# Loading the first activations and weights of a gated MLP in half tiles over two DMA queues

## The chip, the cores and the metric

The kernel runs on one core of one Trainium2 chip. The metric is device time in microseconds (us), lower is better; a program on one core has one value per execution.

A ratio below is the mean time of one kernel's runs over the mean of the other's runs of the same rounds on the same chip. It is therefore not quite the ratio of the medians that stand beside it. Its 95% interval is about 0.0012 to each side with five rounds, which is 0.6 to 0.7 us here. Smaller differences are not told apart by the times, only by what a profile shows.

## The reference

```
x: (1, 2048, 1024) bf16    w_gate, w_up: (1024, 3584)    w_down: (3584, 1024)
g = x @ w_gate ; u = x @ w_up
h = gelu_tanh(g) * u
out = h @ w_down
```

## The kernel before

The kernel is tuned so that TensorE never stops once it has its first operands; its products after the first unit use a scheme with fewer multiplications, which does not matter here. What matters is the head: 512 rows of x come in as four row tiles of 128 rows, are transposed by TensorE, and are multiplied with the first 256 columns of the two weights.

```
def load_x(c):                       # the x issues: 128 rows of 2048 bytes each
    for i in range(NS):              # NS = 4
        xn = slot([P, Dm], bf16, "xn")
        r0 = c * N + i * P
        nc.sync.dma_start(out=xn, in_=x2[r0 : r0 + P, :])
        ...

def load_wf(queue, k0, k1):          # first weights, a part of the contraction at a time
    for i, src in enumerate((w_gate, w_up)):
        got = queue.dma_start(out=wf[:, i, k0:k1], in_=src[k0 * P : k1 * P, 0 : 2 * P]...)
        ...

xT = new_x()
xn0 = load_x(0)
for k0, k1 in ((0, 2), (2, 5), (5, NKB)):
    load_wf(nc.sync, k0, k1)
w = load_w(1)                        # second unit's weights, 512 KB each
for ko in range(NKB):                # x's second 512 rows, transposed by the DMA
    transposing(xT, 1, ko, N)
...
keep_warm(NWARM, N)                  # matmuls on constants until x arrives
for i in range(NS):
    if i == 2:
        keep_warm(2, 2 * P)
    turn(xT, xn0, 0, i)              # 8 transposes of tile i, then a copy into xT
plain(bank[0:4], 0, range(0, 2), parts=2)
plain(bank[0:4], 0, range(2, NKB))
```

Far from the head, the second matrix product fetches its share of w_down per step, the last two steps of each pass in two DMAs:

```
def fetch73(j):
    raw[3, j] = slot([P, 2, N], bf16, "raw")
    for kh in (range(2),) if j < NJ - 2 else (range(1), range(1, 2)):
        kh = slice(kh.start, kh.stop)
        nc.sync.dma_start(out=raw[3, j][:, kh], in_=wdn[:, kh, j, N:])
```

Of the kernel before, what the change touches and what calls it, by code (L numbers as in the profile page):

```python
# [10 lines left out]
def kernel(  # L11
# [23 lines left out]
    nc = tc.nc  # L35
    ENG = mybir.EngineType
    ORDER = {ENG.SP, ENG.DVE, ENG.Pool, ENG.PE}
    P = nc.NUM_PARTITIONS
# [7 lines left out]
    x2 = x.flatten_outer_dims()  # L46
# [7 lines left out]
    NJ = NFB // 2  # L54
    N = 512
# [24 lines left out]
    wdn = w_down.rearrange("(kh j p) d -> p kh j d", kh=2, p=P)  # L80

    def slot(shape, dtype, name):
        return kpool.tile(shape, dtype, name=name, tag="k")
# [33 lines left out]
    def load_w(u, queue=nc.sync):  # L117
        f0 = u * 2 * P
        w = wpool.tile([P, 2, NKB, 2 * P], bf16, name="w")
        for i, src in enumerate((w_gate, w_up)):  # L120
            queue.dma_start(
                out=w[:, i],
                in_=src[:, f0 : f0 + 2 * P].rearrange("(ko ki) f -> ki ko f", ki=P),
            )
        return w
# [160 lines left out]
    q12, s12, q73, q4, raw = {}, {}, {}, {}, {}  # L286
# [24 lines left out]

    def fetch73(j):
        raw[3, j] = slot([P, 2, N], bf16, "raw")
        for kh in (range(2),) if j < NJ - 2 else (range(1), range(1, 2)):
            kh = slice(kh.start, kh.stop)
            nc.sync.dma_start(out=raw[3, j][:, kh], in_=wdn[:, kh, j, N:])

    def make73(j):
        rr = raw[3, j]
# [25 lines left out]
    for j in range(NJ):  # L345
        at(AT12[j], load12, j)
        at(AT12S[j], make12, j)
        at(AT73[j] - 3, fetch73, j)
        at(AT73[j], make73, j)
        at(49 + 0.65 * j, load4, j)  # L350
        at(54 + 0.55 * j, make_sa, j)
# [80 lines left out]
    ident = xpool.tile([P, P], bf16, name="ident")  # L432
    make_identity(nc, ident)

    def load_x(c):
        t = []
        for i in range(NS):
            xn = slot([P, Dm], bf16, "xn")
            r0 = c * N + i * P
            nc.sync.dma_start(out=xn, in_=x2[r0 : r0 + P, :])  # L440
            t.append(xn)
        return t

# [10 lines left out]
            out=xT[c][:, ko, :], in_=x2[r0 : r0 + N, ko * P : (ko + 1) * P]  # L454
        )

    def load_wf(queue, k0, k1):
        for i, src in enumerate((w_gate, w_up)):
            got = queue.dma_start(
                out=wf[:, i, k0:k1],  # L460
                in_=src[k0 * P : k1 * P, 0 : 2 * P].rearrange(
                    "(ko ki) f -> ki ko f", ki=P
                ),
            )
            if queue is not nc.sync:
                tc.keep_in_program_order(got)

    xT = new_x()
    xn0 = load_x(0)
    wf = wpool.tile([P, 2, NKB, 2 * P], bf16, name="w")  # L470
    for k0, k1 in ((0, 2), (2, 5), (5, NKB)):
        load_wf(nc.sync, k0, k1)
    w = load_w(1)
    for ko in range(NKB):
        transposing(xT, 1, ko, N)
# [72 lines left out]
    for ip in range(NPASS):  # L548
# [54 lines left out]
        got, nxt = {}, {}  # L603
# [52 lines left out]
```

## Time and profile before

| | before |
|---|---|
| time, median of 3 (range) | 539.89 us (539.87 to 540.21) |
| the profiled execution | 540.66 us, span 538.8 us |
| TensorE (PE) busy, share of the span | 99% |
| granted TensorE clock from 8 us on | 1.00 |
| fourth x tile landed | 6.99 us |
| first matmul on x | 7.49 us |

The chain of work that ended last, of the kernel before (start in us, length in us, what). It shows where time can be won at all.

```profile
2.12 4.87 DMA xn<-in_x_dram
...
7.04 0.62 PE bank L447 x8
7.66 0.22 PE bank L111 x2
...
7.91 527.77 PE bank L111 x2366
...
535.71 0.58 ACT st L412
```

From 7.91 us to the last copy at 535.71 us the chain is nothing but matmuls. Only the time ahead of 7.91 us can be shortened: the issue and landing of the fourth x tile, its eight transposes (L447), and the wait for w_up.

The x issues by tile, of the kernel before (engine, operation, count, then the length in ns: least, median, most; SPq is SyncE's sequencer):

```profile
L440 SPq DMA_DIRECT2D xn<-in_x_dram x4: 392/420/432, 0.7 to 2.1; - x4
```

The engines' busy times in short stretches, of the kernel before; the last two columns are what is read here, the mean busy share of the 16 DMA engines (it can pass 1, as a packet's whole time counts in the stretch in which it starts) and the GB/s that they moved:

```profile
1.50:2.00 0.50, 0.50 (x2) 0.15 (x1) 0.00 (x0) 0.50 (x1) 0.00 (x0) 1.00 0.24 90
2.00:2.50 0.50, 0.50 (x3) 0.21 (x2) 0.00 (x0) 0.01 (x1) 0.00 (x0) 1.00 0.60 209
2.50:3.00 0.50, 0.50 (x3) 0.22 (x2) 0.00 (x0) 0.00 (x0) 0.00 (x0) 1.00 1.07 324
```

The rate climbs over one microsecond; from 2.5 to 7.5 us it averages above 300 GB/s. That thin start was what a second queue was to fill.

### The profile page before, as it was taken

The page shows a single profiled execution, that of the slowest core. Times are in us where ns is not written, and L with a number is a line of the kernel's source. Part 1 is how long each engine was busy: PE and PEld are TensorE (multiplying, and loading weights), DVE is VectorE, ACT ScalarE, POOL GpSimd, SP SyncE. Part 2 cuts the span into 40 slices and gives each one's busy share as a digit, 9 for nine tenths or more (in the row PEclk, how much of TensorE's full clock was granted, in tenths as well). Part 3 has the DMA queues.
Part 4 walks back from the last instruction along what each step waited for, and adds up shares of the span by engine and source line. Part 5 has one row for each costly group of instructions (what it writes and reads, how often), then busy time and mean ns, then how long its engine had stood idle before and what let it go on. Part 6 is the DMA issues. An engine that isn't in the chain of part 4 may idle for free.

```text
span 538.8 us, 7447 instructions
## 1 busy us (share of the span) xinstructions
PE 534.1 (99%) x2409; PEld 381.2 (71%) x2409; DVE 341.5 (63%) x524; ACT 261.4 (49%) x463; POOL 238.5 (44%) x215
## 2 busy tenths in 40 slices
PE   8999999999999999999999999999999999999997
PEld 5568686867677746888867677676868685488886
DVE  2986766767676894694955455555554649676730
ACT  2556675766666410255355555555555551114431
POOL 1179966677773500000097767676766600000000
DMA  9675656749472999989872223242420049573751
GB/s 243 157 185 168 185 176 175 220 133 260 131 235 72 381 366 297 307 192 296 238 195 80 78 80 88 70 118 63 133 71 9 2 147 390 184 236 96 237 181 51
DMA packets 108198, 93.29 MB, mean 173 GB/s; under 512 B 17280, under 2 KB 93056, under 8 KB 108160
## 3 DMA queue, kind: packets, MB, share of 16 engines
q1 hardware_dynamic: 108160, 92.82, 59.4%
q8 instruction: 19, 0.31, 0.3%
q14 instruction: 19, 0.16, 0.1%
HBM read 74.45 MB, written 15.20 MB: 166 GB/s over the span
## 4 chain that ended last, share of the span: by engine, by line
PE 98%; DMA 1%; SPq 0%; ACT 0%; issue 0%
PE bank L111 98%; DMA xn<-in_x_dram 1%; SPq L440 0%; PE bank L447 0%; ACT st L412 0%
## 5 line engine op out<-in xcount | busy, mean ns | idle before, releaser
L93 POOL TENSOR_TENSOR s<-w 128x512 fp32r<-128x512 bf16 x102 | 119.2, 1189 | 163.2 <-DVE t L90 86.0
L111 PE MATMUL bank<-t,s 128*128 128x512 f32 x648 | 151.7, 390 | 0.0
L111 PEld LDWEIGHTS bank<-t,s 128*128 128x128 f32 x648 | 121.6, 188 | 25.5
L111 PE MATMUL bank<-xT,w 128*128 128x512 bf16 (+1 forms) x504 | 109.7, 376 | 0.0
L107 ACT COPY p<-bank 128x512 f32<-128x512 f32 x124 | 69.9, 590 | 45.4 <-PE bank L111 44.9
L111 PEld LDWEIGHTS <-w 128*128 128x128 bf16 x504 | 48.1, 98 | 58.1 <-issue 3.4
L90 DVE TENSOR_TENSOR hT<-g,bank 128x512 bf16<-128x512 f32 x112 | 76.8, 687 | 17.5 <-PE bank L111 4.5
L90 DVE TENSOR_TENSOR sum<-bank,p 128x512 f32<-128x512 f32 x54 | 37.3, 691 | 79.5 <-PE bank L111 78.4
L179 ACT ACTIVATE g<-sum 128x512 f32<-128x512 f32 x81 | 51.4, 635 | 74.5 <-DVE sum L90 74.2
L111 PE MATMUL bank<-q 128*128 128x512 f32 x240 | 58.9, 389 | 0.0
L93 POOL TENSOR_TENSOR s<-w,s 128x512 fp32r<-128x512 bf16 x50 | 57.7, 1176 | 0.0
L93 POOL TENSOR_TENSOR s<-s,w 128x512 fp32r<-128x512 f32 x50 | 57.2, 1165 | 0.0
L111 PE MATMUL bank<-t,sa 128*128 128x512 f32 x216 | 55.9, 401 | 0.0
L111 PE MATMUL bank<-tb,s 128*128 128x512 f32 x216 | 53.3, 389 | 0.0
L107 ACT COPY u<-bank 128x512 f32<-128x512 f32 x62 | 35.5, 589 | 33.5 <-PE bank L111 33.2
L111 PEld LDWEIGHTS bank<-q 128*128 128x128 f32 x240 | 45.0, 188 | 9.4
L111 PE MATMUL bank<-raw,hT 128*128 128x512 bf16 x224 | 48.7, 379 | 0.0
L102 ACT CAST tb<-raw 128x512 fp32r<-128x512 bf16 x28 | 17.3, 626 | 62.1 <-PE bank L111 27.6
L111 PEld LDWEIGHTS bank<-t,sa 128*128 128x128 f32 x216 | 40.6, 188 | 9.5
L111 PEld LDWEIGHTS bank<-tb,s 128*128 128x128 f32 x216 | 40.5, 188 | 8.4
L90 DVE TENSOR_TENSOR bank<-bank,p 128x512 f32<-128x512 f32 x54 | 37.7, 699 | 8.8 <-PE bank L111 6.2
L90 DVE TENSOR_TENSOR q<-hT 128x512 fp32r<-128x512 bf16 x56 | 38.4, 685 | 4.3 <-PE bank L111 4.3
(44 smaller groups left out, 442.1 us busy)
## 6 DMA issues: line engine op xcount, KB each, us to landing
raw<-in_w_down_dram SPq DMA_DIRECT2D x76, 256.0 KB, 5.0
q<-td SPq DMA_DIRECT2D x60, 256.0 KB, 5.1
w<-in_w_gate_dram SPq DMA_DIRECT2D x27, 512.0 KB, 5.9
w<-in_w_up_dram SPq DMA_DIRECT2D x27, 512.0 KB, 7.0
td<-m SPq DMA_DIRECT2D x12, 768.0 KB, 4.5
w<-td SPq DMA_DIRECT2D x6, 1024.0 KB, 10.0
out_dram<-st SPq DMA_DIRECT2D x32, 128.0 KB, 1.7
td<-w SPq DMA_DIRECT2D x2, 768.0 KB, 6.2
```

Of the source, the lines that this page charges most:

```text
L90: nc.vector.tensor_tensor(out=out, in0=a, in1=b, op=op)
L93: nc.gpsimd.tensor_tensor(out=out, in0=a, in1=b, op=op)
L102: nc.scalar.copy(out=t, in_=src)
L107: nc.scalar.copy(out=t, in_=ps)
L111: nc.tensor.matmul(ps, lhsT=lhs, rhs=rhs, start=start, stop=stop, skip_group_check=True)
L179: nc.scalar.activation(g, src, ACT.Gelu_apprx_tanh)
```

## The change

The intent is to feed the DMA engines from two sequencers at once, so that x and the first weights land sooner. Each x tile is cut into rows 0 to 63 (SyncE's queue) and rows 64 to 127 (ScalarE's queue); the first part of w_up goes to ScalarE's queue. In passing, the last w_down fetches of each pass are merged.

```
     def fetch73(j):
         raw[3, j] = slot([P, 2, N], bf16, "raw")
-        for kh in (range(2),) if j < NJ - 2 else (range(1), range(1, 2)):
-            kh = slice(kh.start, kh.stop)
-            nc.sync.dma_start(out=raw[3, j][:, kh], in_=wdn[:, kh, j, N:])
+        nc.sync.dma_start(out=raw[3, j], in_=wdn[:, :, j, N:])
...
+    def fetch(queue, to, src):
+        got = queue.dma_start(out=to, in_=src)
+        if queue is not nc.sync:
+            tc.keep_in_program_order(got)
...                                                     # in load_x
-            nc.sync.dma_start(out=xn, in_=x2[r0 : r0 + P, :])
+            for queue, p0 in ((nc.sync, 0), (nc.scalar, P // 2)):
+                p1 = p0 + P // 2
+                fetch(queue, xn[p0:p1], x2[r0 + p0 : r0 + p1, :])
...                                                     # in load_wf
-            got = queue.dma_start(...)
+            fetch(nc.scalar if k0 == 0 and i == 1 else nc.sync, wf[:, i, k0:k1], ...)
```

More of the change, by code (lines that the diff above doesn't have):

```diff
@@ L455, in transposing, with load_wf @@
         )
-    def load_wf(queue, k0, k1):
+    def load_wf(k0, k1):
         for i, src in enumerate((w_gate, w_up)):
-            got = queue.dma_start(
-                out=wf[:, i, k0:k1],
-                in_=src[k0 * P : k1 * P, 0 : 2 * P].rearrange(
-                    "(ko ki) f -> ki ko f", ki=P
-                ),
-            )
-            if queue is not nc.sync:
-                tc.keep_in_program_order(got)
+            fetch(
+                nc.scalar if k0 == 0 and i == 1 else nc.sync,
+                wf[:, i, k0:k1],
+                src[k0 * P : k1 * P, 0 : 2 * P].rearrange("(ko ki) f -> ki ko f", ki=P),
+            )
     xT = new_x()
@@ L471 @@
     for k0, k1 in ((0, 2), (2, 5), (5, NKB)):
-        load_wf(nc.sync, k0, k1)
+        load_wf(k0, k1)
     w = load_w(1)
```

## The prediction

> **What bounds the kernel.** The page gives TensorE (PE) 99% busy, and the chain that ended last is 98% matmuls of L111: one unbroken piece from 7.91 to 535.68 us. The windows show PE busy throughout from 8 to 530 us at granted clock 1.00. So only what lies before 7.91 us can be won: the x issues, the fourth x tile's landing (at 6.99), eight transposes (7.04 to 7.66), and a wait until 7.91 for the first w_up.
>
> **The head now.** SyncE needs 0.39 to 0.43 us per x issue and 0.43 to 0.47 us for each first weight half (gate issued at 2.60, up at 3.07). The first packet moves at 1.75 us; the queue moves 90 GB/s in 1.5-2.0 us, 209 in 2.0-2.5, and about 340 from then on. So after 2.5 us the transfers are bound by the DMA engines, not by issuing. In the landings, 15 of the 16 engines had finished x tile 3 at 6.05 and up at 6.94; the sixteenth was some 0.9 us behind, after one packet of 1.5 us.
>
> **What the change does.** The same bytes move; x in eight issues instead of four, four of them by ScalarE, and w_up's first part by ScalarE too.
> - Won: both sequencers feed the engines from 0.74 us on, so the thin start fills: at most about 0.3 us of landing. SyncE loses one issue of 0.47 us.
> - Not won: bandwidth. The Trainium skill, "DMA: Bandwidth & Descriptors", section "Issuing engines are not separate DMA queues", says that DMAs of all issuers run on the same 16 engines and interleave, so a second issuer saves only issue time. The trace's 340 GB/s fits that.
> - New wait: in the trace the ninth DMA waits for the semaphore of the first, the tenth for the second, and so on. With x in eight DMAs, the first gate and up become ninth and tenth, and go out when x tile 0 has landed (about 3.3 us), not at 2.6. Both still stand in the queue before x is through (about 5.3 us): no cost.
> - ScalarE's issues precede its first table load (1.28 us), which then ends near 5 us, in time for its copy of tile 1 (5.46).
>
> **Downstream.** The next tight input, the eighth transposed k-block of x's second half, lands at 22.77; its first matmul starts at 23.48: 0.71 us of slack. An earlier PE uses this up unless the transposes also come earlier; they should, by 0.2 us or more. The merged w_down fetches lie where PE never waits: nothing.
>
> **Sum.** Matmul stream from 7.74 (7.91 less the two matmuls already done) to 7.1-7.4: 0.3 us from the start of the queue, 0.1 to 0.3 from w_up landing with gate instead of 0.43 after it, and up to 0.9 more if the slow engine was an accident of this execution. I predict **539.3 us**, 8 in 10 between 538.4 and 540.0. Faster by over 2%: under 1%. Within 2%: 99%. Slower by over 2%: under 1%.
>
> **In the profile, if right:** over 200 GB/s in 1.5-2.0 us; unchanged near 340 after 2.5; fourth x tile landed by 6.0 to 6.7; gate and up issued at about 3.3 us on two queues, landing within 0.2 us of each other; the unbroken matmul piece starting at 6.7 to 7.4; every engine's busy sum unchanged.
>
> **What would make it wrong.** Two rings per engine moving packets faster or slower than one (over 0.5 us either way); ScalarE's table load standing before its issues, delaying its halves by 1.3 us; the late gate and up issues leaving the engines dry; or the transposes not moving earlier, so that PE waits near 22 us and keeps at most 0.7 us.

## The result, and the profile after

| | before | after |
|---|---|---|
| median of 6 (range) | 540.01 us (539.84 to 540.21) | 541.63 us (541.09 to 542.21) |
| ratio, 95% interval | | 1.003 (1.0017 to 1.0043) |

The change makes the kernel slower by about 1.6 us. That is clear of the noise, within 2%, and outside the predicted range of 538.4 to 540.0. The spread was 0.4 us before and 1.1 us after; in the later rounds the kernel before itself spread by 0.8 to 1.6 us.

The chain that ended last, of the kernel after. The profiled execution took 541.09 us, the quickest of its six.

```profile
0.73 0.58 SPq L434
...
1.37 0.83 SPq L434
...
2.89 4.47 DMA xn<-in_x_dram
...
7.49 0.61 PE bank L452 x8
8.10 528.02 PE bank L111 x2368
...
536.14 0.58 ACT st L410
```

The unbroken piece of matmuls holds two more matmuls than in before (2368 against 2366, the ones that stood at 7.66 there). Their 0.22 us taken off, 528.02 is 527.80 us against 527.77. So between these two executions nothing was lost or won after the head; all of the difference lies ahead of the first matmuls on x.

The x issues by tile, of the kernel after (ACTq is ScalarE's sequencer):

```profile
L434 ACTq DMA_DIRECT2D xn<-in_x_dram x4: 561/611/618, 0.7 to 2.6; - x4
L434 SPq DMA_DIRECT2D xn<-in_x_dram x4: 577/606/830, 0.7 to 2.9; - x4
```

Here is the surprise: to issue half a tile takes 0.56 to 0.83 us, while a whole tile took 0.39 to 0.43. The two sequencers together finish issuing x at 3.50 us, the last one starting at 2.89; the one sequencer of before started its last issue at 2.12 and was done at 2.55.

The same stretches as before, of the kernel after, with one that follows:

```profile
1.50:2.00 0.50, 0.50 (x2) 0.15 (x1) 0.00 (x0) 0.00 (x0) 0.00 (x0) 1.00 0.00 0
2.00:2.50 0.50, 0.50 (x3) 0.21 (x2) 0.00 (x0) 0.00 (x0) 0.00 (x0) 1.00 0.57 156
2.50:3.00 0.50, 0.50 (x3) 0.22 (x2) 0.00 (x0) 0.00 (x0) 0.00 (x0) 1.00 0.97 352
3.00:4.50 1.50, 1.49 (x9) 0.61 (x8) 0.00 (x0) 0.60 (x1) 0.00 (x0) 1.00 0.76 220
```

Nothing at all moves before 2.0 us, and from 3.0 to 4.5 us the engines carry 220 GB/s, where before carried 303 in the first profile and 355 in a second one (below). The thin start did not fill. But by 3.0 us the bytes are nearly level: the rates of these stretches add up to 0.25 MB here, and to 0.28 MB in the second profile of before (57, 98 and 401 GB/s). The shortfall of bytes opens from 3.0 to 4.5 us: 0.33 MB against 0.53.

### The profile page after: what moved, and what is told of

Its sections match the earlier page's. It is cut to its first block, busy times and chain, and to the rows that moved or that the text cites. A ratio compares the mean times of both kernels' runs of the same rounds, so it can differ in the third digit from the quotient of the medians.

```text
span 539.3 us, 7456 instructions
## 1 busy us (share of the span) xinstructions
PE 534.1 (99%) x2409; PEld 381.0 (71%) x2409; DVE 341.8 (63%) x524; ACT 261.1 (48%) x463; POOL 237.9 (44%) x215
## 4 chain that ended last, share of the span: by engine, by line
PE 98%; DMA 1%; SPq 0%; ACT 0%; issue 0%
PE bank L111 98%; DMA xn<-in_x_dram 1%; SPq L434 0%; PE bank L452 0%; ACT st L410 0%
```

## The experiments

The candidate causes that were set against each other: two queues at once are slow, or share the making of descriptors (theories Q and D); half-height DMAs are dear by themselves (H); the weights wait longer because eight semaphores go round, so that the ninth DMA waits for the first to land (R); more and smaller DMAs are the harm (N).

One table for all profiles, read from the issues, the landings and the chain (us). The last column is the execution that was profiled.

| kernel | start of last x issue | fourth x tile landed | first gate, up landed | first matmul on x | last copy | time |
|---|---|---|---|---|---|---|
| before | 2.12 | 6.99 | 7.44, 7.87 | 7.49 | 535.71 | 540.66 |
| before_again | 2.12 | 6.32 | 6.73, 7.11 | 6.83 | 534.97 | 539.93 |
| after | 2.89 | 7.36 | 7.98, 7.78 | 8.02 | 536.14 | 541.09 |
| after_again | 2.90 | 8.06 | 8.72, 8.28 | 9.02 | 537.87 | 542.82 |
| halves_sync | 5.19 | 7.93 | 8.55, 9.31 | 8.60 | 537.48 | 542.43 |
| whole_two | 1.19 | 5.62 | 6.08, 6.98 | 6.43 | 534.87 | 540.19 |
| tiny_scalar | 2.12 | 6.04 | 6.37, 7.37 | 6.55 | 535.20 | 540.44 |
| columns_two | 2.14 | 6.40 | 6.75, 7.14 | 6.79 | 535.13 | 540.05 |
| rows_96_32 | 2.13 | 6.77 | 7.50, 7.07 | 7.55 | 535.58 | 540.54 |

### before_again: the kernel before, for the noise and a second profile

No edit.

> The kernel before, unchanged, for the size of the noise and for a second profile. Theory L (the one slow engine in the first profile of before was an accident): x tile 3 lands near 6.1 us instead of 6.99, the unbroken matmul piece starts at 6.9 to 7.2 instead of 7.91, and the span of the profiled execution is near 538.0 us. Rival (the slow engine belongs to the access pattern): the same engine is again 0.9 us late, x tile 3 lands at 7.0. Time 540.0 in both, ratio 1.000 within 0.0005.

Measured: median 539.93 us (5 runs) against 540.15 (9 runs), ratio 0.9997 (0.9985 to 1.001). The chain of this second profile of before:

```profile
2.12 4.20 DMA xn<-in_x_dram
...
6.37 0.62 PE bank L447 x8
6.99 1.87 PE bank L111 x16
```

One of its stretches:

```profile
3.00:4.50 1.50, 1.50 (x16) 0.82 (x15) 0.15 (x1) 0.00 (x0) 0.00 (x0) 1.00 1.02 355
```

The fourth x tile landed 0.67 us earlier (6.32 against 6.99). The slow sixteenth engine of the first profile was an accident of that execution. This second profile, near the median, is the one to compare with. (About 1% of the matmul records are missing from it, 2388 of 2409, so its chain shows breaks that are no waits; the first profile has all.)

### halves_sync: the half tiles on one queue

```
-            for queue, p0 in ((nc.sync, 0), (nc.scalar, P // 2)):
+            for queue, p0 in ((nc.sync, 0), (nc.sync, P // 2)):
...
-                nc.scalar if k0 == 0 and i == 1 else nc.sync,
+                nc.sync,
```

> The change with all eight half tiles, and the first w_up, on SyncE's queue alone. Theory D (every DMA costs the same descriptor work whatever its height, and the two queues share it): SyncE's issues take about 0.3 to 0.4 us each with nobody beside it, the last x half is issued at about 3.3 us as with two queues, and the time is that of the change, 541.2 to 541.9. Rival Q (two queues at once are the harm, not the halves): 0.2 us per issue, x landed by 6.1, time at or below 540.0. Rival H (half-height DMAs move badly whatever the queue): issues as before at 0.42 us each, engines running dry between 2.5 and 3.5 us, time 541.5 or more.

Measured: 542.84 us (542.43 to 543.89) against 540.15, ratio 1.0055 (1.0041 to 1.0068). The x issues by tile, of halves_sync:

```profile
L434 SPq DMA_DIRECT2D xn<-in_x_dram x8: 575/596/597, 0.7 to 5.2; - x8
```

With nobody beside it, a half tile still takes 0.58 to 0.60 us. So it is not the second queue that makes the issue long, and theory D, which gave 0.3 to 0.4 us here, falls. The slowness belongs to the half-height DMA. Theory H had expected it on any queue, though not that the issue itself would be slow. (Of the time, about 0.2 us is a later wait, for the eighth transposed block of x's second half, which landed at 25.22 us behind the longer row of issues.)

### whole_two: whole tiles on two queues

```
-            for queue, p0 in ((nc.sync, 0), (nc.scalar, P // 2)):
-                p1 = p0 + P // 2
-                fetch(queue, xn[p0:p1], x2[r0 + p0 : r0 + p1, :])
+            fetch((nc.sync, nc.scalar)[i % 2], xn, x2[r0 : r0 + P, :])
```

> The change with whole x tiles, alternating between the two queues (0 and 2 on SyncE, 1 and 3 on ScalarE), the first w_up on ScalarE. Four x DMAs, so the first gate and up wait for nothing. Theory D: issues beside each other take 0.6 to 0.9 us each, in all no sooner than one queue; x is issued by about 2.5 us; time 539.8 to 540.2, as before. Rival Q (two queues moving at once are the harm): 541 or more. If a second queue really helped issuing: x issued by 1.6 us, first packets dense from 1.75 us, time 539.5 or less.

Measured: 540.22 us (539.96 to 540.30) against 540.15, ratio 1.0001 (0.9988 to 1.0013). The x issues by tile, of whole_two:

```profile
L434 ACTq DMA_DIRECT2D xn<-in_x_dram x2: 412/432/453, 0.7 to 1.2; - x2
L434 SPq DMA_DIRECT2D xn<-in_x_dram x2: 392/402/413, 0.7 to 1.2; - x2
```

Two sequencers issue whole tiles side by side as fast as one alone (0.39 to 0.45 us), and x is issued by 1.62 us. Theory Q falls, and D once more. Three stretches of whole_two:

```profile
1.50:2.00 0.50, 0.50 (x2) 0.15 (x1) 0.00 (x0) 0.00 (x0) 0.00 (x0) 1.00 0.85 49
2.00:2.50 0.50, 0.50 (x3) 0.21 (x2) 0.00 (x0) 0.36 (x1) 0.00 (x0) 1.00 0.42 82
3.00:4.50 1.50, 1.27 (x8) 0.36 (x7) 0.00 (x0) 0.42 (x1) 0.00 (x0) 1.00 1.05 406
```

The thin start is still there, with quick issues from two sequencers: 49 and 82 GB/s, against 57 and 98 in the second profile of before. So quick issuing alone does not fill it. The earlier issue won little: the fourth x tile landed at 5.62 against 6.32 us, but up at 6.98 against 7.11, and TensorE waits for up. In the time this agrees with what the prediction quoted from the Trainium skill, that a second issuer saves only issue time. On the rate the profiles do not decide: 406 GB/s from 3.0 to 4.5 us, against 355 in before_again and 386 in tiny_scalar, where x is on one queue.

### tiny_scalar: the longer wait of the weights alone

The kernel before, with a fetch of 2 KB on ScalarE's queue after each x tile:

```
             nc.sync.dma_start(out=xn, in_=x2[r0 : r0 + P, :])
+            tiny = xpool.tile([P // 8, 64], bf16, name=f"tiny{i}")
+            got = nc.scalar.dma_start(out=tiny, in_=x2[r0 : r0 + P // 8, :64])
+            tc.keep_in_program_order(got)
```

> The kernel before, with a fetch of 2 KB on ScalarE's queue after each whole x tile on SyncE's, whose result nobody uses: the DMA count to the first gate is that of the change, so gate becomes the ninth DMA, and gate, up and the later weights wait for x's landings in the rotation of eight semaphores; x itself is as in before. Theory R (that wait is what the change loses): later weights are issued 1 us or more later than in before (third weight issue after 5 us instead of 3.6), the DMA rate falls to about 200 GB/s near 6.5 us, time 541.0 to 542. Rival D (the loss is in the making of x's descriptors alone): gate and up still stand in the queue before x is through, time 540.0 to 540.4.

Measured: 540.49 us (540.02 to 540.64) against 540.15, ratio 1.0005 (0.9993 to 1.0018). Gate was issued at 3.31 us instead of 2.60 and the third weight DMA at 4.26 instead of 3.58; the theory had said after 5. The wait exists and moves the issues, but its cost, if any, is below what these rounds tell apart: at most 1.0 us by the interval, against the 1.6 us of the change. Nothing moved here before 2.0 us either (the first packet at 2.18 us by the packet records), and the fourth x tile still landed at 6.04 us: a late first packet alone is not the loss.

### after_again: the changed kernel, for a second profile

No edit.

> The changed kernel, unchanged, for a second profile nearer its median: time 541.2 to 542.2. Its x issues again 0.56 to 0.62 us for a half tile on either queue, the third weight issue (gate's second part) again after 5.2 us, and the unbroken matmul piece starting 1 to 2 us later than in the repeated profile of before (7.16 us).

Measured: 542.05 us (541.15 to 542.93, 4 runs) against 540.21, ratio 1.0028 (1.0013 to 1.0043). The result repeats, and so do the issues (0.58 to 0.62 us, one 0.84). The third weight issue came at 4.65 us, not after 5.2 as expected; the 5.35 us of the first profile is the latest of the change's four. The profiled execution is a long one of 542.82 us, and it shows a second cost. One stretch of its head, then those around the first matmuls (after the POOL column comes the granted TensorE clock):

```profile
3.00:4.50 1.50, 1.18 (x8) 0.30 (x7) 0.00 (x0) 0.46 (x1) 0.00 (x0) 1.00 1.00 212
...
5.00:6.00 1.00, 0.00 (x0) 0.00 (x0) 0.57 (x1) 0.32 (x1) 0.00 (x0) 1.00 0.99 308
6.00:7.00 1.00, 0.33 (x6) 0.36 (x7) 0.00 (x0) 0.00 (x0) 0.00 (x0) 1.00 1.07 222
7.00:8.00 1.00, 1.00 (x14) 0.94 (x12) 0.00 (x0) 0.68 (x1) 0.00 (x0) 0.68 1.16 242
8.00:9.00 1.00, 1.00 (x12) 0.94 (x10) 0.59 (x1) 0.98 (x2) 0.00 (x0) 0.50 1.14 296
...
10.00:11.00 1.00, 1.00 (x8) 0.73 (x7) 0.02 (x1) 0.00 (x0) 0.00 (x0) 0.62 1.02 288
```

From 3.0 to 4.5 us the engines have a busy share of 1.00 and move only 212 GB/s, where before_again moved 355 at 1.02: the packets take longer here, and a lack of work, as the share of 0.76 in the first profile suggests, is not the whole loss. The other three profiles with 64-row halves on two queues (after_look2, after_look3, after_warm) have shares of 0.87 to 1.05 at 186 to 266 GB/s.

TensorE had nothing to do from 4.8 to 6.67 us, because x tile 1 landed only at 6.54. Then the clock fell to half, from 7.35 to 10.76 us by its records, just when the work came: transposes follow each other at 107 ns instead of 55, the first matmuls at 213 instead of 109. The Trainium skill, "TensorE: Matmul & The Clock Gate", section "Part 1: The HAM clock gate", describes a clock that is halved by windows of 3413 ns, which run freely and watch how busy TensorE was. The trace agrees with the window: its half-clock stretch is 3.413 us long. The same page, section "HAM oscillation — how this bites in real kernels", gives the rule that no idle gap should exceed about 3.4 us; here the clock fell after a gap of 1.83 us. In the window before the fall (3.94 to 7.35 us) TensorE was idle for 2.12 of 3.41 us, and most of its work was transposes; whether these count like matmuls, no run here tests.

### columns_two: halves by columns

```
-            for queue, p0 in ((nc.sync, 0), (nc.scalar, P // 2)):
-                p1 = p0 + P // 2
-                fetch(queue, xn[p0:p1], x2[r0 + p0 : r0 + p1, :])
+            for queue, c0 in ((nc.sync, 0), (nc.scalar, Dm // 2)):
+                c1 = c0 + Dm // 2
+                fetch(queue, xn[:, c0:c1], x2[r0 : r0 + P, c0:c1])
```

> The change with each x tile halved by columns (all 128 rows, 512 columns) instead of by rows. As many DMAs, the same two queues, the same wait of gate and up for the first landings. Theory H (a DMA of 64 whole rows costs 0.58 to 0.60 us to issue on any queue, a DMA of 128 rows 0.39 to 0.45, and the slow issue of x is the larger part of the loss): issues of 0.40 to 0.46 us, x issued by 2.6 us instead of 3.5, x tile 3 landed by 6.2, time 540.2 to 540.8. Rival R (the wait of the weights in the rotation is the larger part): issues quicker, but the third weight issue still after 5 us, time 541.0 or more. Rival N (twice as many DMAs of half the size are the harm): 541 or more with the engines dry near 3 us.

Measured: 540.05 us (539.90 to 540.50) against 540.21, ratio 0.9998 (0.9986 to 1.0011). The x issues by tile, of columns_two:

```profile
L434 ACTq DMA_DIRECT2D xn<-in_x_dram x4: 412/453/454, 0.7 to 2.1; - x4
L434 SPq DMA_DIRECT2D xn<-in_x_dram x4: 392/418/432, 0.7 to 2.1; - x4
```

It has as many DMAs as the change, of the same bytes, on the same two queues, in front of the same wait in the rotation, and the whole loss is gone. (Its profile has a wait of about 0.2 us near 22.7 us, for the eighth transposed block of x's second half, landed at 22.88.) N and R fall as main causes. What is left is the cut by rows, into 64 and 64.

### probe: what an issue costs, by height

The kernel before, with eleven fetches into an unused tile at a moment when SyncE's queue is empty. Each waits until the one that used the same bytes has landed. It slows the kernel, to 561.32 us, and only the issues are read.

```
+        for p0, p1, rows, c1 in (
+            (0, P, x2[0:P], Dm), (0, H, x2[0:H], Dm), (H, P, x2[H:P], Dm),
+            (0, H, x2[0:P:2], Dm), (0, H, x2[0:H], N), (0, P, x2[0:P], N),
+            (0, 96, x2[0:96], Dm), (0, 32, x2[0:32], Dm), (0, 16, x2[0:16], Dm),
+            (0, H, x2[0:H], Dm), (0, P, x2[0:P], Dm)):         # H = 64, P = 128
+            nc.sync.dma_start(out=probe[p0:p1, :c1], in_=rows[:, :c1])
```

> The kernel before with eleven added fetches on SyncE, one behind the other, into a tile that nobody uses, at a moment when its queue is empty: 128 rows; rows 0 to 63; rows 64 to 127; every second row of 128; 64 rows of 512 columns; 128 rows of 512 columns; 96, 32 and 16 rows; 64 rows; 128 rows. Theory H (64 partitions are dear): all fetches to 64 partitions 0.57 to 0.60 us, the others 0.39 to 0.43. Rival C (a source that is one contiguous run short enough to be folded into one dimension is dear): the contiguous 64, 32 and 16 rows, and 64 to 127, are dear; every second row, 64 rows of 512 columns, 128 rows and 128 of 512 columns are cheap; 96 rows tells where the fold ends. Rival B (the queue was busy): all are 0.39 to 0.43. The time is longer by what the fetches hold up, 0 to 20 us, and is not read.

The timeline of SyncE's sequencer in probe (start us, length us). In order: 128 rows; 64 rows; rows 64 to 127; every second row of 128; 64 rows of half the width; 128 rows of half the width; 96, 32 and 16 rows; 64 rows; 128 rows.

```profile
41.19 0.33 SPq L540 DMA_DIRECT2D probe<-in_x_dram  x1
43.92 0.56 SPq L540 DMA_DIRECT2D probe<-in_x_dram  x1
44.53 0.59 SPq L540 DMA_DIRECT2D probe<-in_x_dram  x1
46.51 0.47 SPq L540 DMA_DIRECT2D probe<-in_x_dram  x1
49.17 0.47 SPq L540 DMA_DIRECT2D probe<-in_x_dram  x1
51.49 0.34 SPq L540 DMA_DIRECT2D probe<-in_x_dram  x1
53.69 0.35 SPq L540 DMA_DIRECT2D probe<-in_x_dram  x1
56.16 0.31 SPq L540 DMA_DIRECT2D probe<-in_x_dram  x1
57.97 0.31 SPq L540 DMA_DIRECT2D probe<-in_x_dram  x1
59.67 0.47 SPq L540 DMA_DIRECT2D probe<-in_x_dram  x1
62.17 0.35 SPq L540 DMA_DIRECT2D probe<-in_x_dram  x1
```

All five fetches to 64 partitions take 0.47 to 0.59 us, the others 0.31 to 0.35, whatever their bytes. Both are quicker than expected, in the order of theory H. That the source is one short contiguous run (theory C) is not it: every second row is as dear, and 32 contiguous rows are cheap. The packets tell the same: by their records, the first one of a 64-row fetch moves 1.26 to 1.36 us after the issue began, where the queue was not still busy with another, and 0.95 to 0.99 us after it for the other fetches.

### rows_96_32: cut by rows, but not at 64

```
-            for queue, p0 in ((nc.sync, 0), (nc.scalar, P // 2)):
-                p1 = p0 + P // 2
+            for queue, p0, p1 in ((nc.sync, 0, 96), (nc.scalar, 96, P)):
```

> The change with each x tile still cut by rows over the two queues, but into 96 and 32 rows instead of 64 and 64. Theory H (it is the 64 rows: 0.465 to 0.59 us per issue and a first packet 1.26 us after issue in the probe, against 0.31 to 0.35 us and 0.96 us for 128, 96, 32 and 16 rows): issues of 0.38 to 0.46 us, first packet at 1.76 us, x issued by 2.6 us, time 540.0 to 540.5. Rival R (any cut by rows in two is the harm, for instance because the parts reach the engines unevenly or because the weights then wait in the rotation): 541 or more.

Measured: 540.54 us (540.45 to 540.81) against 540.27, ratio 1.0006 (0.9992 to 1.0019). The x issues by tile, of rows_96_32:

```profile
L434 ACTq DMA_DIRECT2D xn<-in_x_dram x4: 424/440/443, 0.7 to 2.1; - x4
L434 SPq DMA_DIRECT2D xn<-in_x_dram x4: 403/416/426, 0.7 to 2.1; - x4
```

The same change with another cut costs nothing that can be told from the noise. Its median is 0.27 us above that of before and its first matmul on x is at 7.55 us, so a cost of the cut itself, or of the wait in the rotation, is neither shown nor excluded, up to the 1.0 us at which the interval ends. The recovery from the row cut is therefore partly open; that from the cut by columns is clear, as its interval (to 1.0011) ends below that of the change in the same rounds (from 1.0013).

### whole_two_t0: an attempt to beat both

whole_two, with the first transposing fetch ahead of the second unit's weights:

```
+    transposing(xT, 1, 0, N)
     w = load_w(1)
-    for ko in range(NKB):
+    for ko in range(1, NKB):
         transposing(xT, 1, ko, N)
```

> An attempt to beat both: whole x tiles over two queues as in whole_two, and the first of the eight transposing fetches issued ahead of the second unit's weights instead of behind them, so that the transposes end about 1.2 us sooner. If the wait of whole_two near 19 us (0.2 us) and the one that would follow it are what kept its earlier start from showing: 539.5 to 540.0. If the second unit's weights, now later by the transposing issue, are wanted first: 540.2 to 541.5, with a wait near 14 us.

Measured: 540.14 us (540.02 to 540.81) against 540.27, ratio 1.0000 (0.9987 to 1.0012). No gain. The wait "near 19 us" that I wanted to remove was a misreading of mine: the distance of 430 ns there is two matmul steps of 215 ns with a record missing between them, and the chains of before, after and whole_two_t0, whose records are complete, have no wait after the head. A version that beats the kernel before was not found.

### merge_only: the merged w_down fetches

The first hunk of the change, alone.

> The kernel before with the other part of the change alone, the last two w_down fetches of each pass merged into one each. Theory: worth nothing, as TensorE never waits there: ratio 1.000, 539.9 to 540.4, the unbroken matmul piece as long as in before within 0.1 us. Rival: the merged fetch lands later and TensorE waits for it, 540.5 or more.

Measured: 540.68 us (540.46 to 540.77, 4 runs) against 540.27, ratio 1.0007 (0.9993 to 1.002). The median lies in the rival's range (540.5 or more), but the interval includes no change. The times do not settle it; the chain of merge_only does:

```profile
7.58 527.77 PE bank L111 x2366
```

The piece of matmuls is as long as in before, 527.77 us, to the hundredth. In this profile the merged fetches cost nothing and win nothing.

### probe_heights: is it 64 alone

As probe, with other fetches, in order: 128, 112, 80, 64 rows; 64 rows into partitions 32 to 95; 48, 72, 56 rows; 64 rows of 64 columns; 32 rows; 128 rows of 64 columns.

> As probe, with other heights: 128, 112, 80, 64, 64 from partition 32 on, 48, 72, 56 rows, 64 rows of 64 columns, 32 rows, 128 rows of 64 columns. If 64 alone is dear, only the three fetches to 64 partitions take 0.46 us or more. If it is a class of heights (say those below 96 and above 32), then 80, 72, 56 and 48 are dear too. If the dearness comes from the bytes, 64 rows of 64 columns are cheap. The time is not read.

The timeline of SyncE's sequencer in probe_heights:

```profile
...
46.37 0.31 SPq L540 DMA_DIRECT2D probe<-in_x_dram  x1
48.66 0.57 SPq L540 DMA_DIRECT2D probe<-in_x_dram  x1
51.16 0.56 SPq L540 DMA_DIRECT2D probe<-in_x_dram  x1
53.53 0.33 SPq L540 DMA_DIRECT2D probe<-in_x_dram  x1
55.63 0.36 SPq L540 DMA_DIRECT2D probe<-in_x_dram  x1
57.85 0.32 SPq L540 DMA_DIRECT2D probe<-in_x_dram  x1
60.04 0.49 SPq L540 DMA_DIRECT2D probe<-in_x_dram  x1
...
```

Heights 80, 48, 72 and 56 take 0.31 to 0.36 us; 64 takes 0.56 to 0.57, and 0.49 even for 8 KB. By the packet records the first packet moves 1.27 us or more after the issue began for 64 rows, and 0.92 to 0.97 us for the others but one; the fetch of 56 rows has 1.19 us with a quick issue, which stays unexplained. Of the ten heights tried, 64 alone is dear, wherever its partitions start. Why, no profile here shows.

### after_warm, after_look2, after_look3: the spread of the changed kernel

after_warm is the change with work for TensorE's idle time:

```
             turn(xT, xn0, 0, i)
+            if i == 0:
+                keep_warm(4, N)
```

> The change with four matmuls of 512 columns on constants added between the transposes of x tile 0 and tile 1, where TensorE sat idle for 1 to 1.9 us. Theory W (in some executions that idle time lets the clock fall to half for one window of 3.41 us, as in the repeated profile of the change, at clock 0.996 and 542.8 to 542.9 us): no execution above 542.4 and none at a clock below 0.999; the lower level stays at 541.1 to 541.4, as the late x landings stay. Rival: the high executions come from late landings alone, and the spread 541.1 to 542.9 stays.

> The changed kernel, one more profile. If near 541.2: the matmul piece starts near 8.0 us at clock 1.000. If near 542.1 at clock 1.000: x tile 1's second-queue or first-queue half lands near 6.5 us and x tile 3 near 8, the piece starts near 9 us. If near 542.9: as that, with a window of half clock.

> The changed kernel, a further profile, with the same alternatives as the one before it: about 541.2 with the piece from 8.0 us, about 542.1 with the piece from 9 us at full clock, about 542.9 with a half-clock window.

Measured: after_warm 541.08 us (541.02 to 541.30, 5 runs, clock 1.000 in all) against 540.17, ratio 1.0015 (1.0002 to 1.0029). The two looks gave 540.98 and 541.24 us, with the first matmul on x at 7.99 and 8.34 us.

Of all twelve executions of the changed kernel, seven lie at 540.98 to 541.30 us, three at 541.96 to 542.21 and two at 542.82 to 542.93. Those last two have a mean clock of 0.996 and 0.997. With TensorE kept busy all five executions lie in the lowest level. That is what theory W expected of the two highest, and it fits the half-clock window that after_again's profile shows. It is no proof: were each execution high with the odds of 5 in 12, five low ones in a row would come 7 times in 100. The three executions near 542.1 have a mean clock of 1.000, so theory W does not explain them or their absence; none was profiled, and what delayed them stays open.

## Why the prediction was wrong

- **What bounds the kernel: right.** In the first profiles all of the difference lies ahead of the first matmuls; the piece of matmuls is as long as before (527.80 against 527.77 us).
- **The step that failed: "both sequencers feed the engines from 0.74 us on, so the thin start fills: at most about 0.3 us of landing".** It failed twice. It took the issuing for what kept the start thin: whole_two, with quick issues from both sequencers, still moved 49 and 82 GB/s in the stretches from 1.5 to 2.5 us, and its time was that of before (1.0001), so quick issues alone brought no gain. And it took for granted that half a tile is issued at least as fast as a whole one, which turned no gain into a loss. A 64-row half takes 0.56 to 0.83 us instead of 0.39 to 0.43, and its first packet moves later: 2.08 us against 1.78 in the second profile of before, by the packet records. In 1.5 to 2.0 us nothing moved (predicted: over 200 GB/s), from 3.0 to 4.5 us 220 GB/s (second profile of before: 355). The fourth x tile landed at 7.36 and 8.06 us (predicted: 6.0 to 6.7; second profile of before: 6.32). columns_two and rows_96_32, which differ from the change in the shape of the halves alone, bring the time back to 540.05 and 540.54. So the 64-row halves are the cause, shown best by columns_two. By which way they cost the time is in part open: the later issues of x (done at 3.50 us instead of 2.55) and slower packets from 3.0 to 4.5 us go together in these runs, and why packets were slower no run shows.
- **The start point was also off.** The sum began at the 7.74 us of a profiled execution that was 0.77 us slower than the median, and counted "up to 0.9" us as a possible win "if the slow engine was an accident". It was one, but the typical times of before had never held it, so nothing of it could be won. An execution near the median has its first matmul on x at 6.83 us (before_again), not at 7.49.
- **The new wait in the rotation: it is there, and it cost nothing that can be told.** Gate and up were issued at 3.81 and 3.46 us in the first profile (predicted: about 3.3) and landed within 0.20 us of each other, as predicted (0.44 in after_again). tiny_scalar (1.0005) and columns_two (0.9998) have the wait and not the loss. In the change itself the wait is longer, as it follows the late landings of x: the third weight issue is at 4.60 to 5.35 us in four profiles, against 4.26 and 4.07 in those two. How much of the loss passes through this, the runs do not separate.
- **No bandwidth from a second queue: not contradicted.** whole_two had x issued by 1.62 us and the same time as before; its rate after 3.0 us is too near that of one queue (406 against 386 GB/s in tiny_scalar) to decide.
- **The next tight input, the eighth transposed block: right.** TensorE waited about 0.2 us for it in columns_two and in halves_sync.
- **The table load of ScalarE: right.** It ran from 3.90 to 5.18 us, ahead of the copy at 6.45.
- **The merged fetches: right**, by the length of the piece of matmuls in merge_only.
- **Not foreseen:** TensorE's longer idle time between x tiles 0 and 1 can cost a window of half clock: shown for one execution by its profile, and likely for the other at 0.997. With after_warm the mean over before is 0.15%, against 0.3% for the change, but the intervals overlap (1.0002 to 1.0029 and 1.0017 to 1.0043): how much of the mean loss goes when TensorE is kept busy is not measured. The loss in the lowest level, about 0.9 us, stays.

## What to carry to other kernels

Before cutting a DMA over two queues, look at the issue time of the exact shape in a trace: in the probes here a fetch to 64 partitions cost 0.12 to 0.26 us more to issue than one to 128, and began to move 0.3 to 0.4 us later, and in the kernel eight halves were slower than four wholes. If a load must be cut in two, try a cut by columns (0.9998) or at another height (1.0006). Before you count on a second issuer, check that issuing is what holds the start back. Check also whether the profiled execution is a typical one before you add up what can be won from it, and look for idle time of TensorE while the first loads come in late.

## What the Trainium skill lacked or had wrong

- "DMA: Bandwidth & Descriptors" and the other pages have no word on an issue being dearer for exactly 64 partitions: 0.47 to 0.59 us in the probes, against 0.31 to 0.36 us for 16, 32, 48, 56, 72, 80, 96, 112 and 128, and a first packet 1.26 us or more after the issue against 0.92 to 0.99 us for the others but 56 (1.19 us).
- The same page, section "Rules for kernel authors", advises against two transfers to disjoint partition halves because they share the engines, and for one 128-partition transfer. The advice holds here, as no cut gained time; what the page does not say is that the even cut loses some (1.003), while the cut at 96 and 32 rows cost nothing clear (1.0006) and a cut by columns nothing (0.9998).
- The same page, section "Issuing engines are not separate DMA queues", agrees with the times: whole tiles on two queues were issued by 1.62 us instead of 2.55, and the time stayed (1.0001).
- "TensorE: Matmul & The Clock Gate", section "HAM oscillation — how this bites in real kernels": the rule against idle gaps over about 3.4 us was not enough here. The half-clock window of 3.413 us followed a gap of 1.83 us, in a window of which TensorE was idle for 2.12 us, seen in one execution. As most of the work in that window was transposes, this does not show the rule wrong for matmuls.
